# One more head pair transposed by the DMA crossbar in a block-sparse attention + gated conv FFN kernel, with a new written-out order

## The chip, the cores and the metric

One core of a Trainium2 chip. The metric is the device time of one execution in microseconds (us), as the median of several runs.

## The reference: what is computed

Attention with a block mask over q, k, v of shape [4 batches, 8 heads, 768 tokens, 64], then a feed-forward block on the result. The shape of the work, cut to what matters:

```python
scores = (1 / sqrt(64)) * q @ k^T                    # masked to -1e9 outside the allowed 32x32 blocks
attn   = softmax(scores)                             # window, first/last block row and column, 3 sampled blocks
x      = (attn @ v) as [4, 768, 8*64]
h      = relu(x @ w_in)                              # 512 -> 1024
gate   = sigmoid(conv over 3 tokens of h, per channel)
out    = (h * gate) @ w_out                          # 1024 -> 512
```

The kernel computes all 768 x 768 scores; the mask is added inside the score product by 24 extra rows (one for each block of 32 tokens) under the 64 rows of head data, which is why the score products read 88 partitions.

## The kernel before, in words

**Pairs.** The 32 (batch, head) combinations are handled as 16 *pairs* of two heads, four pairs to a batch. A pair's q and k must stand transposed (head dimension on the partitions) in a slot `t` (`T_t`, five slots, [88, 24, 128]): rows 0 to 63 are data, rows 64 to 87 the mask. Columns 0 to 11 hold q, 12 to 23 hold k.

There are two ways to fill a slot. Pairs below `NPE` (line 136) go by `kq_transposes` (line 429 on): TensorE transposes k (six products of 128 columns, L475), the first half of q (three, L537) and later, from a separate load `nq`, the second half of q (three more, L537), each into a PSUM bank `mix`, and copies on DVE or ACT (L328, L324) carry them into the slot. Pairs from `NPE` on go by `kq_crossbar` (line 568 on): k and all of q are loaded into `nat`, the SP queue issues two crossbar transposes (L612, `DMA_TRANSPOSE`) into a staging tile `stg` (two of them), and two copies of 64x1536 on DVE (t<-stg, L328) fill the slot. For such a pair the mask rows stand in another order, so SP also issues one DMA that turns them (t<-mback), from a tile `mback` that two earlier DMAs on SP filled.

**Units.** The score work is cut into 144 units of eight 128x128 blocks. In a unit TensorE makes the scores (S, L774) into one of two PSUM tiles `st`, ACT takes the exponential of all 1024 columns (L786) into `pt` (six buffers), and TensorE multiplies with v (AV, L811, eight products of 65 columns) into `av`. After every few units DVE normalises (`rcp` L720, `xtok` L722), the result is transposed to `xT` by TensorE (L741) or the crossbar (L731), and the feed-forward work runs: f1 = x @ w_in (L919) into `mix`, relu on ACT (L939) or DVE (L941) into `hE`, three multiplications (L977) and two additions (L985) for the conv on DVE, tanh on ACT (L1024), +1 (L1027) and the gate product (L1032, `gT`) on DVE, f2 = gated h @ w_out (L849) into `mix`, eviction to `o2s` (L324 on ACT, L328 on DVE) and the store by SP (L862). A store of a block that is listed in `OUT_TWO` is issued as two DMAs.

**The head.** While the first loads run, TensorE makes 13 warm-up products of 256 columns and 29 *fills* of 128 columns (L230, `warm`) at points where it would wait. DVE builds the mask: it needs the sampled block numbers (`sbi`), makes `A` and `mtok` (L296) and copies mask rows into slot 0. It also sets the column of ones that stands beside each v slot (`v_one`, memset of `vt`, L372, one for each of five slots) and copies q and k into the slot. The first q and k are loaded as float32 and cast: the second q cast, that of head 1, is done by POOL (L326 CAST). POOL also issues the casting loads of the other pairs (L239).

**What sets the order.** All operations are recorded in a graph, but nothing schedules them when the program is built: the text `ORDER` lists every operation in the order in which it is emitted, with the engine where there is a choice and the number of each buffer. Each engine runs its own instructions in that order. An operation that waits holds up all that stand behind it on its engine. `SEQ` is the chain of POOL's middle loads (nq5 is the second half of pair 5's q).

Of the kernel before, what the change touches and what calls it, by code (L numbers as in the profile page):

```python
# [20 lines left out]
0J1f0O0I0K1k0L0002103040M05010P1W01X060Q1U0070R281080S0+A1EA21CA1FA29090/V13G150N181b0a1g0b1h0c1i0d1j0e0U0f0V0g0XV  # L21
1G01HA00YV12G1DG16G2610h1M10i0j0k1NV1IV0l1J01KA191c1LV0m0n0o0p5b05c5g15h0q0r1O00s5d05i10T1PV0t0u1Y11ZV11+V0v5l05m
5n20w1/020V21V1VV05q15r5v00x0y5s35w5x40z5e05f5j5E15F5k1m10A0W0ZV1n1Q02m32n22114V5G55J05K2a00B0C2bV25L00D5O10E5P2d1
0F0G5o5T02cV5Q12eV2fV27V12k22g22y02A24V2B4W2u31w4X2M14Y2O01x4Z2P4+5U5p5t0H5V25u5y5A06015B616231R05z15H6501SV1TV66
2o16742pV32qV5I6a16b2r05M5N5R6f06g2sV2tV6c52lV25S5W5X6k16l5C1230630645Y11l1d24V25V5Z5DV02zV36h06m16t06u68696y16z6d
6v26e6i6A36j6D06E5+02h16n6o16I16J6F46w6x6B6R06C6S6G6H6K56L6M6W16X6T06Y15/V6p22iV2jV6q6N06r0176O6sV6/06U0706P16V6QV
1a71274175763iR0iS7907aiU1iV7i17j7b42NV4iTV00iWVjd07k51y4/2+26Z6+7n07oiX0iY7s17t7p0jejfjgiZV1501z5130152jh7273i+1i/
7x07y7u1j0A1e103217z22v07G177787H7c7d12wV2xVjl1j712C07l7m7L07Mjn2DV47e12EV7I3ji7N47qj87Q1j9V27r7R2F07v7w7S57f2GV2HV
jm7V07W2Q17A7+17/j107Bjj2RV07X0801870887J08927K7O7P8c18d7Tj27U8h07C2jo2SVjpj3V38e38i7Y2T17Z8m181j408j4jq2/V07D2UV
2VV830330jk08n8o531531A348v0j5j6Vjr8wja1821jbjcVjt2jB384ju8x08a8A18B7E08b8f8g7g18C17hA18F08k8G8l8H28p8K18q8y08L851  # L30
8z8M38P08D8Q8R48E8I8J8N8X18Y8r2jD86V8sjw8t18O7FVjvjC8uVjs35VjxjE8Z58S90091jJ0951969208T18+jKjP19719a08/9b93jQjy36V
jF541B55370jz9c2jGjA11jH563939i194989j999n09d9ejR9ojL9k43b23c1573a3d9p59s19t9u1583g13i3j23l592I05a3u3k3r8U1jI9f0
38V13hV2jSjTV0jM9x09yjNA19g3eV3fV8V9z3jV1jWjXA9l1jY0jZ9C19Dj+A2J19K09L9mj/0k09E09P19Q9q9M29R49r9v2KVkh0kik1Vkk2LVkj
9w9U09V9A9B9Fk209H2kl9W59Ik3k4Akp1km9G09Z19+9/1kqa50k51k809Nk9k63n08W23v02W1krknk7Vksa6kaAa739Oaa19Sabac0ke02X19T
af0ag9Xkf9Yak1alah4kx22YVky2ZVkAktam5kb1ap0kca0aqa1a81a9adax1aeaiajay3x3s23w3G3DkukzkdVa21kgVkokvkF3a3kBkwkGkHkIar2
anaz1aoaC0aDaskT1aH1aIat0aAaE3aJ0kCaBaM0aFaNaGl30aU1aKl4aLkUaVaO4aZ0aPaQa+kJkKaW5a/2kDkEkVl5b219h9J3o3z13A3m3a43y4
au0kLkMkWb3l6kXA2b433pV3BVl7V3avb70lc1b8ldb90l903CV3qVbc1aX1labdaYlbV14leAbe53H13E03J3I3S3P3Q13T33Vbk0blli1b0lf0bm1
b1ljb5lkAlx0aR2lyaSlAlzlBlglhA5lF1lH3tV3b6bp1bqbr4ball1bu0bblC3L1jOkYl83M3W0aw03K0aT3Ubvlo0lmlnV6bz1bw2bAbfbg0lpbn
bolqAbB3bsbH0lr1bIbtbxlsbM1bybNlu0bJ0ltA7lGlN2lOlQlDbR0bCbSlvkN1bO5bh1lIbilwV3FV43NVlE1lJlV3bW1bXbT1bY4kZ0bDkOb/0
bK13RA0bE0lPbFlWlRc0c71c8c13k+bLbPbQbUk/bVbZb+c90lKcc0cdkPl0ce53Xl1A1bGbjl2jUlYlLlXlZkQc2c30cach1cbcikRV2lS3+41422  # L40
3/24643lMc42lTl+l/3OVlUcj2m70m11cm0cnm8m2cu1cvcw1co4m3m9m03YV1mambV3cz1m4m5V1cAcfcB3cE0mg0cFmhmd13ZVc540V1miVcG0me
# [71 lines left out]
def kernel(  # L113
# [28 lines left out]

# [76 lines left out]
    OUT_TWO = ((0, 1), (0, 2), (1, 0), (1, 1), (1, 2))  # L219
# [679 lines left out]
    for n, (b, g, tok, C, _) in enumerate(SEGS):  # L899
# [4 lines left out]
        w1 = 128 * C  # L904
# [176 lines left out]
```

## Time and profile before

| | us |
|---|---|
| median of 3 runs | 206.12 |
| lowest, highest run | 205.99, 206.56 |
| the profiled execution | 205.24 |
| its span, first to last instruction | 203.5 |
| time of the profiled execution outside its span | 1.7 |

The profiled execution was 0.88 us faster than the median. Times in the trace are counted from the start of the span. The matmul rows overlap: a product of 128 columns is shown with about 0.22 us, but the next one starts 0.055 us later, so what a product costs TensorE is read from start to start. TensorE's granted clock is 1.000 of full speed.

### The profile page before, as it was taken

To read this page: it belongs to the slowest core of one execution; us is meant where nothing else is said; L and a number is where in the kernel's file an instruction comes from. 1 tells how busy PE (TensorE), PEld (TensorE's weight loads), DVE (VectorE), ACT (ScalarE), POOL (GpSimd) and SP (SyncE) were. 2 spreads that over 40 slices of the span, in tenths; PEclk is the share of its full clock that TensorE was granted. 3 is DMA by queue.
4 is the path that set the end of the run, shared out by engine and by line. 5 is a ranking of instruction groups with operands and counts; after the bars stand their busy time and mean duration, and the time that the engine had idled before them with its cause. 6 is when DMAs were issued, how large, how long until landed. Compare 5 with 4: busy or idle time off the path is not lost.

```text
span 203.5 us, 6346 instructions
## 1 busy us (share of the span) xinstructions
PE 198.4 (98%) x2442; PEld 144.5 (71%) x2442; DVE 183.7 (90%) x576; ACT 189.2 (93%) x251; POOL 68.0 (33%) x148
## 2 busy tenths in 40 slices
PE   7899999999999999999999999999999999999994
PEld 5688878887677766766477676766667657887773
DVE  7789789999999998999899998999999988999961
ACT  6899999999999999999799998999999989998861
POOL 8995646434271504114115443873000000000000
DMA  6999999999789996999948799994005222000315
GB/s 140 178 169 199 184 201 159 159 154 149 72 92 176 113 140 88 241 143 136 175 60 109 138 148 155 186 216 91 0 30 177 82 75 99 3 0 5 133 46 185
DMA packets 50986, 25.45 MB, mean 125 GB/s; under 512 B 35588, under 2 KB 48884, under 8 KB 50956
## 3 DMA queue, kind: packets, MB, share of 16 engines
q0 software_dynamic: 20000, 11.24, 43.6%
q1 hardware_dynamic: 30632, 13.63, 33.2%
q8 instruction: 19, 0.31, 0.6%
q10 hardware_dynamic: 324, 0.18, 0.3%
q14 instruction: 11, 0.09, 0.1%
HBM read 23.09 MB, written 6.29 MB: 144 GB/s over the span
## 4 chain that ended last, share of the span: by engine, by line
PE 93%; DVE 3%; ACT 2%; issue 1%
PE st L774 31%; PE mix L919 21%; PE mix L849 19%; PE av L811 17%; PE mix L741 1%; PE st L849 1%; DVE t L328 1%; PE mix L537 1%; PE mix L475 1%; ACT o2s L324 1%; PE av L996 1%; ACT m L1024 1%; PE av L230 1%; ACT pt L786 1%; DVE mtok L296 0%
## 5 line engine op out<-in xcount | busy, mean ns | idle before, releaser
L786 ACT ACTIVATE pt<-st 128x1024 bf16<-128x1024 f32 x144 | 140.6, 1032 | 3.3 <-PE st L774 2.2
L774 PE MATMUL st<-t 88*128 88x256 bf16 (+2 forms) x600 | 93.3, 267 | 0.8 <-ACT pt L786 0.4
L811 PEld LDWEIGHTS <-pt 128*128 128x128 bf16 x1152 | 55.7, 97 | 12.4
L811 PE MATMUL av<-vt,pt 128*128 128x65 bf16 x1152 | 62.7, 193 | 0.0
L774 PEld LDWEIGHTS <-t 88*128 88x128 bf16 x600 | 48.0, 97 | 20.5 <-DVE t L328 1.0
L919 PE MATMUL mix<-xT,winb 128*128 128x384 bf16 (+2 forms) x288 | 55.2, 307 | 0.1
L977 DVE TENSOR_SCALAR m<-hE,cw 128x382 bf16<-128x382 bf16 (+2 forms) x192 | 50.2, 318 | 0.3 <-ACT hE L939 0.2
L849 PE MATMUL mix<-woutb,gT 128*128 128x512 bf16 (+2 forms) x200 | 49.4, 360 | 0.0
L985 DVE TENSOR_TENSOR m<-m 128x764 bf16<-128x764 bf16 (+2 forms) x64 | 33.6, 531 | 0.2
L919 PEld LDWEIGHTS <-winb 128*128 128x128 bf16 x288 | 23.7, 97 | 8.5 <-issue 0.5
L1024 ACT ACTIVATE m<-m 128x764 bf16<-128x764 bf16 (+2 forms) x32 | 26.3, 825 | 0.1
L849 PEld LDWEIGHTS <-gT 128*128 128x128 bf16 x224 | 18.8, 97 | 9.0 <-DVE gT L1032 0.3
L420 POOL COPY pace<-pt 1x1 bf16<-1x1 bf16 x24 | 8.4, 348 | 50.0 <-ACT pt L786 49.8
L939 ACT ACTIVATE hE<-mix 128x384 bf16<-128x384 f32 (+2 forms) x37 | 18.1, 502 | 0.6 <-PE mix L919 0.4
L1032 DVE TENSOR_TENSOR gT<-m,hE 128x764 bf16<-128x764 bf16 (+3 forms) x36 | 18.1, 510 | 0.7 <-ACT hE L939 0.4
L722 DVE TENSOR_TENSOR xtok<-av,rcp 128x384 bf16<-128x384 f32 (+2 forms) x36 | 18.2, 508 | 0.4
L239 POOL DMA_DIRECT2D nat<-in_q_dram x23 | 17.0, 739 | 3.1 <-issue 2.2
L941 DVE TENSOR_SCALAR hE<-mix 128x384 bf16<-128x384 f32 x27 | 15.0, 554 | 2.6 <-PE mix L919 2.3
L328 DVE COPY t<-mix 64x384 bf16<-64x384 bf16 (+1 forms) x34 | 14.0, 411 | 1.6 <-PE mix L475 0.6
L1027 DVE TENSOR_SCALAR m<-m 128x764 bf16<-128x764 bf16 (+3 forms) x36 | 12.0, 336 | 1.2 <-ACT m L1024 0.9
L324 ACT COPY o2s<-mix 128x512 f32<-128x512 f32 (+2 forms) x17 | 9.3, 549 | 3.8 <-PE mix L849 3.7
L239 POOL DMA_DIRECT2D vn<-in_v_dram x16 | 12.0, 748 | 0.9 <-issue 0.3
(76 smaller groups left out, 124.6 us busy)
## 6 DMA issues: line engine op xcount, KB each, us to landing
out_dram<-o2s SPq DMA_DIRECT2D x16, 256.0 KB
vn<-in_v_dram POOLq DMA_DIRECT2D x16, 192.0 KB, 5.0
nat<-in_k_dram POOLq DMA_DIRECT2D x15, 192.0 KB, 4.6
out_dram<-o2s SPq DMA_DIRECT2D x15, 128.0 KB
nat<-in_q_dram POOLq DMA_DIRECT2D x6, 192.0 KB, 4.2
winb<-in_moe_w_in_dram POOLq DMA_DIRECT2D x2, 512.0 KB, 7.2
woutb<-in_moe_w_out_dram POOLq DMA_DIRECT2D x4, 256.0 KB, 6.8
nat<-in_q_dram POOLq DMA_DIRECT2D x9, 96.0 KB, 5.3
```

Source lines behind the costliest of these rows:

```text
L239: return op(name, {eng: occ}, lambda e: on(e).dma_start(out=dst(), in_=src), prio, deps, dma=(kind, service), **kw)
L722: nm = op("norm", {"DVE": t_dps(128 * C)}, lambda e: nc.vector.tensor_tensor(out=xtok_t[xk.index][:, 0:C].rearrange("p c h d -> p h c d"), ...
L774: nc.tensor.matmul(out=st[:, 128 * x:128 * (x + n_)], lhsT=t[0:88, 12 + 6 * hh + kc, :], rhs=t[0:88, idx:idx + (n_ - 1) * (2 if P < NPE el ...
L786: nc.scalar.activation(out=pt_t[ptb.index][:, c0:c1], in_=st_t[stb.index][:, c0:c1], func=AF.Exp, bias=0.0, scale=0.125)
L811: nc.tensor.matmul(out=o[:, off:off + 65], lhsT=pt_t[ptb.index][:, 128 * x:128 * x + 128], rhs=V_t[vslot_b[P].index][:, hh, kc, 0:65], sta ...
L849: nc.tensor.matmul(out=acc(), lhsT=gT_t[gb.index][:, ffc, 128 * t:128 * t + 128], rhs=woutb[:, ffc, c0:c1], start=(ffc == 0), stop=(ffc == ...
L919: nc.tensor.matmul(out=mix_t[hb.index][:, w1 * y:w1 * y + w1], lhsT=winb[:, fc, 128 * ffc:128 * ffc + 128], rhs=xT_t[xt_buf[n].index][:, f ...
L939: nc.scalar.activation(out=dst, in_=src, func=AF.Relu, bias=0.0, scale=0.5)
L977: nc.vector.tensor_scalar(out=m_t[cb.index][:, x, y, 0:w], in0=hE_t[heb.index][:, f0 + y, t0 + x:t0 + x + w], scalar1=cw[:, x, f0 + y:f0 + ...
L985: nc.vector.tensor_tensor(out=m[:, a_, :, 0:w], in0=m[:, a_, :, 0:w], in1=m[:, b_, :, 0:w], op=ALU.add)
L1024: th = [op("tanh", {"ACT": t_act(2 * w) + 0.04}, lambda e, cb=cb, w=w: nc.scalar.activation(out=m_t[cb.index][:, 0, :, 0:w], in_=m_t[cb.in ...
L1032: nc.vector.tensor_tensor(out=gT_t[gtb.index][:, f0:f0 + 2, t0:t1], in0=m_t[cb.index][:, 0, :, 0:w], in1=hE_t[heb.index][:, f0:f0 + 2, 1 + ...
```

## The change

1. `NPE` goes from 6 to 5: pair 5 goes by `kq_crossbar`, and `nq5` leaves `SEQ`.
2. `OUT_TWO` loses (1, 1) and (1, 2): those two stores are one DMA each.
3. `ORDER` is written anew from the first line on.

```diff
-    NF, NPE = 4, 6
+    NF, NPE = 4, 5
...
-    SEQ = "nq0 nq1 nq2 k4 q4 nq3 v4 k5 q5 w0 v5 w1 k6 q6 w2 w3 v6 k7 q7 v7 nq4 nq5"
+    SEQ = "nq0 nq1 nq2 k4 q4 nq3 v4 k5 q5 w0 v5 w1 k6 q6 w2 w3 v6 k7 q7 v7 nq4"
...
-    OUT_TWO = ((0, 1), (0, 2), (1, 0), (1, 1), (1, 2))
+    OUT_TWO = ((0, 1), (0, 2), (1, 0))
...
-0J1f0O0I0K1k0L0002103040M05010P1W01X060Q1U0070R281080S0+A1EA21CA1FA29090/V13G150N181b0a1g0b1h0c1i0d1j0e0U0f0V0g0XV
+0J1f0O0I0K1k0L0002103040M05010P1W01X060Q1U0070R281080S0+A1EA21CA1FA090/V13G150N181b0a0b0c0d0e0U0f0V0g0XV1G01HA00YV
...
```

What the new order does on the engines, counted over the whole program: TensorE has 12 transposes and their 12 weight loads fewer; DVE makes six `t<-mix` copies fewer (four of 64x384, two of 64x768), two more `t<-stg` and one more `vt<-vn`, and one relu fewer; ACT makes one relu more and the copy `vt<-vn` no longer; SP issues two crossbar transposes more and two stores fewer (with both halves of a store counted). Three places that the prediction speaks of follow, with a fourth in a sentence; `+` and `-` mark rows that only the changed or only the old kernel has there.

On DVE, at the very head: `nblk` and the first mask rows of slot 0, then the four later memsets of ones (`vt1` to `vt4`), `A` and `mtok` from the sampled blocks `sbi`, and below, after the first copies into slot 0 (the row with `av0` is one of them):

```order
 L328 COPY t0_67<-nblk_125 24x3x128
-L372 MEMSET vt1_73 128x12
-L372 MEMSET vt2_74 128x12
-L372 MEMSET vt3_75 128x12
-L372 MEMSET vt4_76 128x12
 L296 SCALAR_TENSOR_TENSOR A_130<-sbi_126,keyid_129,A_130 24x24 x2
 L296 SCALAR_TENSOR_TENSOR mtok_131<-sbi_126,keyid_129,A_130 24x384
```

The four memsets moved behind the mask and the first copies into the slot; they now stand ahead of the copy of head 1's first q.

On POOL, at the head: loads of pair 0's v (`vn0`) and of pair 2's k (`nat1`), two copies of mask rows inside slot 0, the cast of head 1's q of pair 0 (`nat2<-o2s0`) and the load of pair 2's q:

```order
 L239 DMA vn0_87<-in_v_dram 128x2x384
 L239 DMA nat1_80<-in_k_dram 128x2x384
-L239 DMA nat1_80<-in_q_dram 128x2x192
 L326 COPY t0_67<-t0_67 24x768
 L326 COPY t0_67<-t0_67 24x3x128
 L326 CAST nat2_81<-o2s0_113 128x192
+L239 DMA nat1_80<-in_q_dram 128x2x192
 L326 COPY t1_68<-t0_67 24x6x128
```

The load's issue moved behind the cast; the copies and the cast moved up by one issue.

On SP, in the first third, pair 5's crossbar transpose of k (`stg0<-nat0`) now stands ahead of the last mask copy (slot 4) and of the two DMAs that fill `mback`, that of its q behind them, and the turn of its mask rows (`t0<-mback`) behind the first crossbar transpose of pair 6.

On DVE, around the first use of pairs 10 and 11: four copies from the staging tiles into slots `t0` and `t1`, among the +1 rows (L1027, which wait for ACT's tanh), the gate products (L1032) and evictions to `o2s`. Before, where slot 0 holds pair 10:

```order
L1027 TENSOR_SCALAR m2_109<-m2_109 128x2x382
L1027 TENSOR_SCALAR m3_110<-m3_110 128x2x382
L328 COPY t0_67<-stg1_78 64x12x128
L1032 TENSOR_TENSOR gT1_112<-m2_109,hE1_106 128x2x382
L1032 TENSOR_TENSOR gT1_112<-m3_110,hE1_106 128x2x382
L328 COPY t1_68<-stg0_77 64x12x128
L328 COPY o2s3_116<-mix0_65 128x512
```

And now, where slot 1 holds pair 10:

```order
L1027 TENSOR_SCALAR m2_109<-m2_109 128x2x382
L328 COPY vt0_72<-vn1_88 128x12x64
L720 RECIPROCAL rcp0_99<-av0_63 128x6
L328 COPY t0_67<-stg0_77 64x12x128
L328 COPY t1_68<-stg1_78 64x12x128
L1032 TENSOR_TENSOR gT1_112<-m2_109,hE1_106 128x2x382
L328 COPY t1_68<-stg1_78 64x12x128
L1027 TENSOR_SCALAR m3_110<-m3_110 128x2x382
```

The last copy for pair 10 stood behind the +1 row of `m3`; it now stands ahead of it, but behind pair 11's first copy.

More of the change, by code (lines that the diff above doesn't have):

```diff
@@ L20 @@
 ORDER = """
-0J1f0O0I0K1k0L0002103040M05010P1W01X060Q1U0070R281080S0+A1EA21CA1FA29090/V13G150N181b0a1g0b1h0c1i0d1j0e0U0f0V0g0XV
[L22 to L40, printed above, removed]
@@ L61 @@
+qT0hPi71i8hQqoquqPAgqvqy1qUqzi95hI1qpqAr20qwhR2qxqVAhhJr4r3hSri2rjr5qBqK0qLhY0hZi01i1qCA3qMAii30i21iaibhK1hLA2i4qQ0
+i51qRi6AqSAjic1qW1rlqXr6idrkqZqYra3q+rbrcqE1qFhT0qGhUAie0qHifAqIA0rI0rJrKArO1rPq/r0rdr1rQAr7rU0rVrL0rMrNArR1s21rSs3
+rW1rTArq0rZ0r8rerfqJqDpzopr9rmrXrYrw1r+s40rnr/1s5rgrhrxrrs71ros0s1rpsA0s8s93sasu1rsrysvsBsbs6rzrtswrAA0ruA3sc1sxsC
+rC0sDrDrEsyA2rFsdsEArGArBszrvsFrHsesfsi0sjskslso1sgA1shsmAsnspsqsrssAst
 """
```

55 lines of the change are left out of this document (35 added, 20 removed).

## The prediction

> **What bounds the kernel now.** I read the page first, then the stretches by time, then the chain of work that ended last, and last the instructions around the places where that chain leaves TensorE.
>
> ```profile
> PE 198.4 (98%) x2442; PEld 144.5 (71%) x2442; DVE 183.7 (90%) x576; ACT 189.2 (93%) x251; POOL 68.0 (33%) x148
> PE 93%; DVE 3%; ACT 2%; issue 1%
> ```
>
> TensorE (PE) is busy for 98% of the 203.5 us span, and 93% of the chain that ended last is its work. But ACT at 93% and DVE at 90% leave little room, so the shares alone do not say who sets the pace. The next rows are from the view of stretches: start and end, length, then busy time with number of instructions for PE, weight loads, DVE, ACT and POOL, the granted clock, the DMA share and GB/s.
>
> ```profile
> 8.50:24.50 16.00, 15.55 (x265) 13.24 (x263) 13.37 (x39) 15.94 (x17) 12.60 (x23) 1.00 1.28 186
> 24.50:45.00 20.50, 20.48 (x291) 15.91 (x289) 18.96 (x55) 20.36 (x25) 8.94 (x20) 1.00 1.21 170
> 45.00:90.00 45.00, 45.00 (x550) 31.89 (x549) 43.21 (x127) 44.68 (x56) 14.97 (x28) 1.00 1.02 136
> 90.00:180.00 90.00, 89.77 (x1055) 62.15 (x1054) 85.21 (x265) 86.46 (x114) 24.05 (x63) 1.00 0.61 108
> ```
>
> From 8.5 to 45 us ACT is full (15.94 of 16.00, 20.36 of 20.50): the exponentials run back to back. From 45 to 180 us TensorE is full and ACT has 3.9 us to spare (135.00 less 44.68 and 86.46). So work taken from TensorE pays in full only where it is the bound, and a start of the exponentials that comes sooner pays in the first part. The chain by time says where it leaves TensorE: up to 9.6 us in the head, at the end, and in between at one place alone (start, length, what):
>
> ```profile
> 94.56 0.57 ACT o2s L324
> 95.12 0.40 ACT m L1024
> 95.75 0.85 ACT m L1024
> 96.62 0.36 DVE m L1027
> 97.01 0.81 DVE t L328
> 97.86 0.33 PEld L774 LDWEIGHTS <-t 88*128 88x128 bf16 x4 [0.72 <-DVE t L328]
> 97.87 0.61 PE L774 MATMUL st<-t 88*128 88x384 bf16 x4 [0.23 <-DVE t L328]
> 98.58 1.02 ACT L786 ACTIVATE pt<-st 128x1024 bf16<-128x1024 f32 x1 [1.07 <-PE st L774]
> ```
>
> The last three rows are from the timeline, with the idle time before them in brackets. Pair 10's last copy into its slot (97.01) stands on DVE behind a +1 row that waits for tanh. The scores wait for the copy, with 0.23 us of TensorE idle, and ACT then idles for 1.07 us.
>
> **Part 1: pair 5 leaves TensorE.** The transposes that go, in the timeline of TensorE, each followed by what starts next:
>
> ```profile
> 35.76 0.50 PE L475 MATMUL mix<-ident,nat 128*128 128x128 bf16 x6
> 36.10 0.28 PE L811 MATMUL av<-vt,pt 128*128 128x65 bf16 x4
> 39.62 0.33 PE L537 MATMUL mix<-ident,nat 128*128 128x128 bf16 x3
> 39.78 0.28 PE L811 MATMUL av<-vt,pt 128*128 128x65 bf16 x4
> 57.40 0.33 PE L537 MATMUL mix<-ident,nq 128*128 128x128 bf16 x3
> 57.56 0.60 PE L774 MATMUL st<-t 88*128 88x256 bf16 x4
> ```
>
> From start to next start they take 36.10 - 35.76 = 0.34, 39.78 - 39.62 = 0.16 and 57.56 - 57.40 = 0.16 us: **0.66 us** of TensorE. Nine of the twelve lie ahead of 45 us, where ACT is the bound; there the room lets TensorE take feed-forward products forward, which are then missing from the full stretch behind. I take all 0.66 us; the ends are 0 (ACT keeps the pace and nothing is taken forward) and 0.66.
>
> The Trainium skill speaks against this part: the page "VectorE: DVE Perf Modes", section "Rules for kernel authors", says to transpose 128x128 on TensorE where PSUM will do, and its section "The three transpose paths" gives 390 ns there and 1309 ns on the crossbar. By 390 ns the twelve would be 4.7 us of TensorE, an estimate from that page; the trace's 0.055 us from start to start decides against counting so.
>
> The copies change too:
>
> ```profile
> L328 DVE COPY t<-stg 64x1536 bf16<-64x1536 bf16 x20 | 11.6, 586 | 0.2
> L328 DVE COPY t<-mix 64x384 bf16<-64x384 bf16 x24 | 8.4, 351 | 0.8 <-PE mix L537 0.4
> L328 DVE COPY t<-mix 64x768 bf16<-64x768 bf16 x10 | 5.5, 555 | 0.8 <-PE mix L475 0.6
> L324 ACT COPY vt<-vn 128x768 bf16<-128x768 bf16 x1 | 0.8, 837 | 0.0
> ```
>
> DVE loses four of 351 ns and two of 555 ns and gets two of 586 ns: 1.40 + 1.11 - 1.17 = 1.34 us less. ACT loses one copy of 837 ns to DVE. The other moves between the two are single relus and evictions, and nearly cancel. So no engine gets more work; I count nothing for these, since neither is the bound where TensorE is full, and they are the cover for the rest of the new order.
>
> On SP and the DMA engines two crossbar transposes come in. Their cover is time. The first row below is the first crossbar transpose of pair 6, the second the first score product that reads pair 5's slot, the third all crossbar transposes of that line (min, median, max of the issue in ns):
>
> ```profile
> 34.41 3.38 SPq L612 DMA_TRANSPOSE stg<-nat  x2
> 45.60 0.38 PE L774 MATMUL st<-t 88*128 88x128 bf16 x2
> L612 SPq DMA_TRANSPOSE stg<-nat x20: 1210/1237/2307, 34.4 to 138.1; - x20
> ```
>
> The last thing that pair 5 now needs from SP, the turn of its mask rows, stands right behind pair 6's first transpose, so it is issued at about 34.41 + 1.24 = 35.7 us, and 45.60 - 35.7 = 9.9 us are left for its way and for two copies of 0.59 us. I cost it at nothing; what it costs when that cover is gone is the rival below.
>
> **Part 2: the head.** The chain there, and what POOL does beside it:
>
> ```profile
> 3.54 0.23 DVE vt L372 x4
> 3.80 0.26 DVE A L296
> ...
> 5.89 1.03 PE st L774 x8
> ...
> 7.04 0.03 issue
> 7.06 0.35 PE av L515 x3
> ...
> 8.56 1.03 ACT pt L786
> 4.50 0.72 POOL L239 DMA_DIRECT2D nat<-in_q_dram  x1
> 5.26 1.34 POOL L326 COPY t<-t 24x768 bf16<-24x768 bf16 x2
> 6.67 0.34 POOL L326 CAST nat<-o2s 128x192 bf16<-128x192 f32 x1
> ```
>
> The four memsets of ones stand on the chain itself, and `A` is not shown waiting for its load, so without them the mask, the copies into slot 0, the first scores (5.89) and the first exponential come 0.23 us sooner. It could be nothing, if the load of the block numbers landed just before 3.80, or 0.26 with the gap between rows; I take 0.23. The second step must not eat it: unit 2 needs head 1's q, whose transposes (7.06) wait for POOL's cast (ends 7.01). The issue of 0.72 us that goes behind the cast lets the cast end up to 0.72 sooner; the two fills that now stand behind the score products of units 0 and 1 run into the time that this leaves. TensorE reaches these transposes 0.23 sooner and finds the data there. The memsets now run on DVE before head 1's copy, in time in which DVE waits for those transposes. So all exponentials of the full stretch begin **0.23 us** sooner.
>
> The load that moved is pair 2's q. Its landing, in us after its issue, that of nine other loads of its size, and its first use:
>
> ```profile
> nat<-in_q_dram POOLq DMA_DIRECT2D x1, 96.0 KB, 7.0
> nat<-in_q_dram POOLq DMA_DIRECT2D x9, 96.0 KB, 5.3
> 12.98 0.33 PE L537 MATMUL mix<-ident,nat 128*128 128x128 bf16 x3
> ```
>
> It landed at 4.50 + 7.0 = 11.5, and is now issued behind two copies and a cast, at 4.50 + 1.34 + 0.34 and the gaps, about 6.3. If the 7.0 us were its own, it would land at 13.3 and TensorE, which now comes by at 12.75, would stand for 0.55 us; if it is the queue of loads ahead of it, it lands at 11.5 as before. Nine loads of that size take 5.3 us in the median, so part of the 7.0 is queue, and with 6.3 + 5.3 = 11.6 it would be there in time: I take 0, and keep 0.55 for the range.
>
> **Part 3: the rest.** At pair 10 the copy no longer waits for the last tanh, but has pair 11's copy of 0.59 us ahead of it in place of a +1 of 0.36. The gain ends at the 0.23 us that TensorE idled, the loss at the 0.59 us of that copy; I take 0. Two stores as one DMA each: SP waits most of the time, nothing. The other hundreds of moves I can't price one by one; since each engine has less work and TensorE's stream is otherwise the same, I take 0 and keep 0.6 us on either side, the size of the one hole that the chain shows (0.23 on TensorE, 1.07 on ACT; about the mean of the two).
>
> **Sum.** 0.66 + 0.23 = 0.89 us less than the profiled execution: 205.24 - 0.89 = 204.35 us, span 202.6. The median of the runs shown is 0.88 above that execution, so 206.12 - 0.89 = **205.2 us**.
>
> **The rivals.**
>
> *ACT keeps the pace.* Most of pair 5's transposes lie where ACT is full, and if the new order takes no other TensorE work forward, the 0.66 is lost: 206.12 - 0.23 = 205.9 us. For it speaks the full ACT up to 45 us; against it that 0.16 us of them lie behind, and that ACT gets no more work while TensorE's part behind 45 us is a fixed sum from which each product done earlier is taken.
>
> *A slot comes late through SP (slower).* SP issues in order, and a store or a transpose that waits holds up every crossbar transpose behind it. The view of waits shows how long:
>
> ```profile
> SPq L862 <- ACT o2s L324: 21.7, 8, 12.1
> ```
>
> Eight waits of stores for an eviction, the longest 12.1 us. With two transposes more and another order on SP, such a wait can now stand ahead of a pair's transposes or of its mask rows. From a wait of 9.9 us on, the cover worked out above for pair 5, each us of it is a us that TensorE stands; at 12.1 it is 12.1 - 9.9 = 2.2 us, and 205.2 + 2.2 = 207.4 us. Against it speaks that such waits lay ahead of transposes before too, and no slot came late.
>
> *More than the sum.* If the new order also closes the hole at 97 us and some of what ACT lost there, up to 0.6 us more goes: 204.6 us.
>
> **How the numbers follow.** The forecast has 0.47, more than the sum 0.15, ACT's pace 0.20, the late slot or another hole of its size 0.18. 0.3% is 0.62 us here, about what a measurement of this kernel can tell from no change: faster means below 205.5 us. The first two cases make faster 0.62, the third the same 0.20, the last slower 0.18. The range reaches down to 205.2 - 0.6 - 0.5 = 204.1 (the unknown moves and the spread of the three runs, 0.57) and up to 206.9, where the 0.66 is lost, pair 2's q costs its 0.55 and 0.6 us of new waits come in (205.9 + 0.55 + 0.6 = 207.05, of which I leave out the last bit); that leaves out most of the late slot.
>
> **What would show it.** No L475 or L537 rows between 36 and 42 us, and no three L537 rows near 57 us; `A` at about 3.55 us, the first scores at 5.65, the first exponential at 6.3; TensorE's L537 for pair 2 without idle time at about 12.75; no wait of L774 for t<-stg before 60 us; the stretch from 45 to 180 us shorter for the same units. Wrong would be: `A` still at 3.8, an idle TensorE behind a crossbar copy, or ACT idle for more than a us anywhere between 10 and 180 us.

## The result, and the profile after

The changed kernel is slower: 207.25 us as the median of 22 executions (204.72 to 212.21) beside 205.86 for the kernel before (205.33 to 206.75). The ratio is 1.0034, with a 95% interval of 1.0018 to 1.0051. Like all ratios below it leaves out executions more than 1.5% above the fastest of the same kernel; the eight of the changed kernel that go by this (208.38 to 212.21) ran at a granted clock of 0.99 to 1.00, so they belong to what the change costs, and the plain quotient of the two medians is 1.0068.

The changed kernel also spreads over 7.5 us, the one before over 1.4. The profiled execution took 209.0 us, its span 207.2. Busy times and the chain that ended last, from its page:

```profile
PE 198.7 (96%) x2430; PEld 144.1 (70%) x2430; DVE 181.7 (88%) x572; ACT 189.9 (92%) x251; POOL 67.1 (32%) x146
...
PE 65%; DMA 18%; DVE 11%; issue 2%; ACT 2%; POOL 1%; SPq 0%; DVEq 0%; POOLq 0%
...
L328 DVE COPY t<-stg 64x1536 bf16<-64x1536 bf16 x22 | 12.0, 549 | 3.2 <-DMA stg<-nat 2.9
```

The counts are as they were worked out: 12 products fewer on TensorE, four instructions fewer on DVE. What is new stands in the second row: of the chain, 18% are now DMA, and TensorE has 65% in place of 93%. The third row is the copy from the staging tile on DVE, which now stands idle for 2.9 us in all, at two places, because a crossbar transpose has not landed.

The same stretches as before, in the same columns:

```profile
8.50:24.50 16.00, 15.53 (x263) 13.13 (x260) 14.11 (x38) 15.89 (x18) 13.06 (x26) 1.00 1.34 194
24.50:45.00 20.50, 19.73 (x268) 15.05 (x265) 16.70 (x48) 19.90 (x24) 7.17 (x17) 1.00 1.35 153
45.00:90.00 45.00, 43.97 (x554) 31.48 (x552) 42.53 (x126) 43.23 (x55) 17.34 (x41) 1.00 1.07 151
90.00:180.00 90.00, 87.99 (x1023) 60.60 (x1022) 81.93 (x253) 84.80 (x109) 22.44 (x48) 1.00 0.65 105
```

TensorE is no longer full in any of the last three: it lacks 0.77, 1.03 and 2.01 us, where it lacked 0.02, 0.00 and 0.23. The second last column, the DMA share, is the time of all packets over the time of the core's 16 DMA engines; it passes 1 where packets overlap. Below, "full" DMA engines are those of the first two stretches, where it is 1.2 and more. Where TensorE stood, the view of what it waited for says (us in all, how often, the longest). The first and the last row stand in the kernel before too:

```profile
PE av L230 <- DVE warm L223: 1.2, 1, 1.2
PE mix L919 <- DMA xT<-xtok: 1.0, 1, 1.0
PE st L774 <- DMA t<-mback: 1.0, 1, 1.0
PE mix L919 <- DVE hE L941: 0.9, 1, 0.9
PE mix L919 <- DVE t L328: 0.7, 1, 0.7
PE st L774 <- ACT pt L786: 0.4, 1, 0.4
```

The four new waits come to 3.6 us, and 209.0 - 3.6 = 205.4 us is what is left. Two of them stand at pair 5, in rows of the timelines of DVE and TensorE:

```profile
40.70 0.55 DVE L328 COPY t<-stg 64x1536 bf16<-64x1536 bf16 x1 [1.14 <-DMA stg<-nat]
...
42.19 0.48 PE L919 MATMUL mix<-xT,winb 128*128 128x384 bf16 x2 [0.69 <-DVE t L328]
...
48.00 0.38 PE L774 MATMUL st<-t 88*128 88x384 bf16 x2 [0.99 <-DMA t<-mback]
```

Pair 5's copy waits 1.14 us for its crossbar transpose; a copy out of a PSUM bank stands behind it on DVE (41.77 us in the chain), and f1 waits 0.69 for that bank. Later the scores stand 0.99 us for the turn of pair 5's mask rows. SP's own rows show how that came:

```profile
25.13 1.40 SPq L612 DMA_TRANSPOSE stg<-nat  x1
26.63 0.81 SPq L239 DMA_DIRECT2D t<-t  x1
27.50 1.62 SPq L340 DMA_DIRECT2D mback<-t  x2
29.57 2.48 SPq L612 DMA_TRANSPOSE stg<-nat  x1
39.02 0.81 SPq L239 DMA_DIRECT2D t<-mback  x1
40.91 1.23 SPq L612 DMA_TRANSPOSE stg<-nat  x1
42.24 0.81 SPq L239 DMA_DIRECT2D t<-mback  x1
```

The first transpose of pair 5 waits for its k until 25.13, and behind it stand the fills of `mback` (27.50; before they were issued at 13.03). The transpose of its q, issued at 29.57, is shown in the chain with 11.03 us until it lands at 40.60. The turn of pair 5's mask rows is the last row, at 42.24, behind pair 6's first transpose at 40.91; it lands 5.71 us later, at 47.95. The prediction had put these two at 34.41 and 35.7. Pair 6's transpose waits for pair 6's load of k. Its landing, in us after its issue at 30.1 (changed) and at 30.5 (before), is the row on which most of what follows hangs:

```profile
nat<-in_k_dram POOLq DMA_DIRECT2D x1, 192.0 KB, 10.8
```

```profile
nat<-in_k_dram POOLq DMA_DIRECT2D x1, 192.0 KB, 3.9
```

### The profile page after: what moved, and what is told of

It is laid out like the page before. It is cut to its first block, busy times and chain, and to the rows that moved or that the text cites. A ratio compares the mean times of both kernels' runs of the same rounds, so it can differ in the third digit from the quotient of the medians.

```text
span 207.2 us, 6306 instructions
## 1 busy us (share of the span) xinstructions
PE 198.7 (96%) x2430; PEld 144.1 (70%) x2430; DVE 181.7 (88%) x572; ACT 189.9 (92%) x251; POOL 67.1 (32%) x146
## 4 chain that ended last, share of the span: by engine, by line
PE 65%; DMA 18%; DVE 11%; issue 2%; ACT 2%; POOL 1%; SPq 0%; DVEq 0%; POOLq 0%
PE st L774 20%; PE mix L849 16%; PE mix L919 14%; PE av L811 10%; DMA stg<-nat 8%; DMA nat<-in_q_dram 7%; DMA t<-mback 3%; DVE t L328 2%; DVE m L985 2%; DVE m L977 2%; ACT pt L786 1%; PE st L849 1%; DVE hE L941 1%; DVE xtok L722 1%; PE av L996 1%
## 5 line engine op out<-in xcount | busy, mean ns | idle before, releaser
L786 ACT ACTIVATE pt<-st 128x1024 bf16<-128x1024 f32 x144 | 140.2, 1034 | 4.3 <-PE st L774 3.4
L811 PEld LDWEIGHTS <-pt 128*128 128x128 bf16 x1152 | 54.9, 97 | 12.9
L811 PE MATMUL av<-vt,pt 128*128 128x65 bf16 x1152 | 61.7, 193 | 0.0
L420 POOL COPY pace<-pt 1x1 bf16<-1x1 bf16 x24 | 8.9, 372 | 43.8 <-ACT pt L786 42.2
L941 DVE TENSOR_SCALAR hE<-mix 128x384 bf16<-128x384 f32 x26 | 14.3, 554 | 7.2 <-PE mix L919 7.0
L1032 DVE TENSOR_TENSOR gT<-m,hE 128x764 bf16<-128x764 bf16 (+3 forms) x36 | 18.2, 511 | 0.4
L239 POOL DMA_DIRECT2D nat<-in_q_dram x23 | 17.7, 770 | 2.0 <-issue 1.9
L328 DVE COPY t<-stg 64x1536 bf16<-64x1536 bf16 x22 | 12.0, 549 | 3.2 <-DMA stg<-nat 2.9
L328 DVE COPY t<-mix 64x384 bf16<-64x384 bf16 (+1 forms) x28 | 11.5, 410 | 1.8 <-PE mix L475 0.8
L1027 DVE TENSOR_SCALAR m<-m 128x764 bf16<-128x764 bf16 (+3 forms) x36 | 11.8, 332 | 1.2 <-ACT m L1024 0.7
L239 POOL DMA_DIRECT2D vn<-in_v_dram x16 | 11.4, 715 | 2.9 <-DVE vt L328 1.7
```

Source lines behind the costliest of these rows:

```text
L239: return op(name, {eng: occ}, lambda e: on(e).dma_start(out=dst(), in_=src), prio, deps, dma=(kind, service), **kw)
L328: nc.vector.tensor_copy(out=dst, in_=src)
L786: nc.scalar.activation(out=pt_t[ptb.index][:, c0:c1], in_=st_t[stb.index][:, c0:c1], func=AF.Exp, bias=0.0, scale=0.125)
L811: nc.tensor.matmul(out=o[:, off:off + 65], lhsT=pt_t[ptb.index][:, 128 * x:128 * x + 128], rhs=V_t[vslot_b[P].index][:, hh, kc, 0:65], sta ...
```

## The experiments

**The theories.** *A: the landing.* Two crossbar transposes among full DMA engines delay the loads and DMAs around them by microseconds, and with the order in which SP has its instructions this makes slots late. *B: DVE's order*: the copies hold up what stands behind them. *C: the head*: moving the load or the memsets costs what the transposes gain. *D: nothing but the transposes on TensorE counts*, so they gain less than the sum or nothing. Each experiment is one part of the change done to the kernel before, or one part of it undone. The rows with `+` and `-` are the instructions in order on the engine named.

### The memsets alone: h_ones

The kernel before, with only the four memsets of ones moved, on DVE:

```diff
-L372 MEMSET vt_73 128x12
-L372 MEMSET vt_74 128x12
-L372 MEMSET vt_75 128x12
-L372 MEMSET vt_76 128x12
 L296 SCALAR_TENSOR_TENSOR A<-sbi,keyid,A 24x24 x2
...
 L286 CAST ident_123<-ident 24x24
+L372 MEMSET vt_73 128x12
...
 L328 COPY t_67<-av_63 64x3x128
```

> The kernel before with only the four memsets of ones moved behind the first copies into slot 0; POOL's load stays in front. Port theory (a DVE copy from SBUF waits while a copy of POOL is running): A at 3.47, the copy from mtok starts at about 4.68 and takes 0.32 since POOL's copy starts only at 5.26, first scores at 5.56 in place of 5.89, third exponential at 8.2 to 8.3 in place of 8.56; the time 0.2 to 0.3 us lower (ratio 0.9985 to 0.999). Rival (the head is held by something else that the memsets hide): first scores stay at 5.8 to 5.9, ratio 1.000.

Measured: 205.73 us (205.13 to 206.13) beside 205.68, ratio 1.0002 (0.999 to 1.0013). `A` comes at 3.47 in place of 3.80, as the prediction had it, yet the first scores come at 6.52 us, later than the 5.89 of before. TensorE's rows, of this kernel and then of the kernel before, show why:

```profile
4.91 0.53 PE L515 MATMUL mix<-ident,nat 128*64 128x128 bf16 x3
5.37 0.61 PE L230 MATMUL av<-warm 128*128 128x128 bf16 x4
5.77 0.53 PE L475 MATMUL av<-ident,nat 128*128 128x128 bf16 x3
```

```profile
4.75 0.35 PE L515 MATMUL mix<-ident,nat 128*64 128x128 bf16 x3
5.03 0.40 PE L230 MATMUL av<-warm 128*128 128x128 bf16 x4
5.27 0.33 PE L475 MATMUL av<-ident,nat 128*128 128x128 bf16 x3
```

Four products of 128 columns take 5.77 - 5.37 = 0.40 us here, 5.27 - 5.03 = 0.24 there: 0.10 and 0.06 apiece, for the same instructions. So in the first microseconds TensorE goes at about half speed for a time that differs between executions, though the column of the granted clock reads 1.00. The Trainium skill, page "TensorE: Matmul & The Clock Gate", section "What's actually happening", tells of a gate that lets half the clock pass until a window of about 3.4 us has been busy. These rows agree in the factor (0.10 to 0.055 us); when the switch comes varies: in a_sp three products take 0.18 us from 4.38 on, in p5_alone2 four still take 0.42 us from 6.10 on. What the memsets give is thus hidden behind TensorE in some executions, and in the median nothing of it is seen.

### The load alone: h_load

The kernel before, with only the issue of pair 2's q moved behind the second cast on POOL:

```diff
-L239 DMA nat_80<-in_q_dram 128x2x192
 L326 COPY t_67<-t_67 24x768
 L326 COPY t_67<-t_67 24x3x128
 L326 CAST nat_81<-o2s_113 128x192
+L239 DMA nat_80<-in_q_dram 128x2x192
```

> The kernel before with only the issue of pair 2's q moved behind POOL's cast. Port theory: POOL's first copy starts at 4.55, before DVE's copy from mtok (5.01), and holds it to about 5.5; first scores at 6.05 to 6.1 in place of 5.89, third exponential at 8.7 to 8.8; the time 0.2 us higher (ratio 1.001). Rival (the prediction's step: the earlier cast only helps): first scores at 5.89, ratio 1.000 or a little below.

Measured: 205.81 us (205.65 to 206.24), ratio 1.0010 (1.0001 to 1.0019): a loss of about 0.2 us. The move lets POOL's copy of mask rows begin 0.7 us sooner, and there it meets DVE's copies of 24x256. POOL, DVE and the first scores of this kernel, then DVE of the kernel before:

```profile
4.56 1.10 POOL L326 COPY t<-t 24x768 bf16<-24x768 bf16 x1
...
5.01 0.93 DVE L328 COPY t<-mtok 24x256 bf16<-24x256 bf16 x2
...
6.38 1.03 PE L774 MATMUL st<-t 88*128 88x384 bf16 x8 [0.48 <-DVE t L328]
```

```profile
5.01 0.45 DVE L328 COPY t<-mtok 24x256 bf16<-24x256 bf16 x2
```

The two copies on DVE take 0.93 in place of 0.45 us, and the first scores wait for the copy behind them. The changed kernel shows the same (POOL's copy at 4.55, DVE's two at 4.68 with 0.97), and its first scores come at 6.08; in a_all2 below, where the load is back in front, the two take 0.58 us and the first scores come at 5.81. The page "SBUF — State Buffer" of the Trainium skill, section "Who interferes with whom", says that DVE and GpSimd share a pair of ports as an exclusive lock, and that where an instruction of DVE uses the pair, the one that issues first holds the other off; 0.93 beside 0.45 agrees.

### Pair 5 alone, in two orders: p5_alone and p5_alone2

The kernel before with pair 5 by the crossbar and nothing else of the change; SP fills `mback` early and turns pair 5's rows at once.

```diff
-    NF, NPE = 4, 6
+    NF, NPE = 4, 5
...
-    SEQ = "nq0 nq1 nq2 k4 q4 nq3 v4 k5 q5 w0 v5 w1 k6 q6 w2 w3 v6 k7 q7 v7 nq4 nq5"
+    SEQ = "nq0 nq1 nq2 k4 q4 nq3 v4 k5 q5 w0 v5 w1 k6 q6 w2 w3 v6 k7 q7 v7 nq4"
```

> The kernel before with only part 1: pair 5 by the crossbar, in the old order, its transposes right behind the fills of mback on SP, its two copies on DVE just ahead of the unit that first reads the slot. The prediction's term of 0.66 us: ratio 0.9965 to 0.9975. ACT keeps the pace: 0.999 to 1.000. If the crossbar's way is too slow even from there (11 us from issue to landing as in the changed kernel's profile): TensorE idles before unit 40 and the ratio is over 1.003.

Measured: 206.99 us (206.34 to 207.57), ratio 1.0063 (1.0043 to 1.0083). TensorE's timeline has one long new wait, the second row; the first is DVE's:

```profile
43.83 1.11 DVE L328 COPY t<-stg 64x1536 bf16<-64x1536 bf16 x2
...
46.73 0.28 PE L811 MATMUL av<-vt,pt 128*128 128x65 bf16 x4 [1.01 <-DVE xtok L722]
```

Here the two copies from staging stand in one piece ahead of a normalisation (`xtok`). p5_alone2 takes them apart, on DVE:

```diff
+L328 COPY t_67<-stg_78 64x12x128
 L941 TENSOR_SCALAR hE_105<-mix_65 128x384
 L1027 TENSOR_SCALAR m_108<-m_108 128x2x382
+L328 COPY t_67<-stg_78 64x12x128
 L941 TENSOR_SCALAR hE_105<-mix_66 128x384
-L328 COPY t_67<-stg_78 64x12x128 x2
```

> Pair 5 alone by the crossbar in the old order as in p5_alone, but its two copies on DVE apart, in the two gaps of 0.62 and 0.53 us ahead of relus that wait for TensorE, in place of both ahead of the xtok that held TensorE for 1.17 us. If that wait was only the place of the copies, it goes and the ratio comes down by 0.004 to 0.006. Then by the prediction's term of 0.66 us: ratio 0.997; by the rival that ACT keeps the pace up to 45 us: 0.999 to 1.000. If the ratio stays above 1.003, the crossbar's way costs more than its place on DVE.

Measured: 206.29 us (205.69 to 206.67), ratio 1.0025 (1.0011 to 1.0039). The wait is gone, and with it 0.7 us, so B was true of p5_alone. But pair 5 alone, with no such wait left, is still slower than before by 0.25%, outside both forecasts above (0.997, 0.999 to 1.000). TensorE's one new wait (0.20 us, in p5_alone too) is for ACT, behind the place where six of the transposes stood. Below it, the landing of pair 6's k in this kernel:

```profile
36.92 0.60 PE L774 MATMUL st<-t 88*128 88x128 bf16 x4 [0.20 <-ACT pt L786]
```

```profile
nat<-in_k_dram POOLq DMA_DIRECT2D x1, 192.0 KB, 8.2
```

It takes 8.2 us in place of 3.9, but no wait of TensorE in this execution hangs on it. Where the time goes, and that the transposes give so little, is taken up below, at x_twice.

### SP's order undone: a_sp, and the changed kernel again

a_sp is the changed kernel with SP's order mended: the mask copy and the fills of `mback` ahead of pair 5's transposes, and pair 5's turn ahead of pair 6's transpose.

```diff
-L612 DMA_TRANSPOSE stg_77<-nat_79 128x6x128
 L239 DMA t_71<-t_67 24x3072
 L340 DMA mback<-t_67 24x3x128 x2
-L612 DMA_TRANSPOSE stg_77<-nat_79 128x6x128
+L612 DMA_TRANSPOSE stg_77<-nat_79 128x6x128 x2
+L239 DMA t_67<-mback 24x2x768
 L239 DMA t_68<-mback 24x2x768
 L612 DMA_TRANSPOSE stg_78<-nat_80 128x6x128
-L239 DMA t_67<-mback 24x2x768
 L612 DMA_TRANSPOSE stg_78<-nat_80 128x6x128
```

> The changed kernel with one difference on SP: the slot 4 mask copy and the two fills of mback ahead of pair 5's crossbar transposes, and pair 5's mask turn ahead of pair 6's. Theory (pair 5's mask rows come late because these small DMAs stand behind a transpose that waits 16 us for k): the turn is issued by 36 us, TensorE does not wait for t<-mback at 47 us; median 1 to 2 us below the changed kernel's 207.25 (ratio to the kernel before 0.996 to 1.001) and a narrower spread than its 204.7 to 212.2. Rival (the slow crossbar landing of 11 us itself is what makes pair 5 late): a wait of about the same size for t<-stg in its place, ratio 1.003 to 1.006 and the same spread.

Measured: 205.83 us (204.52 to 210.55), ratio 1.0000 (0.9978 to 1.0021), where the change had 1.0034. Both waits at pair 5 are gone:

```profile
13.39 1.63 SPq L340 DMA_DIRECT2D mback<-t  x2
26.61 4.80 SPq L612 DMA_TRANSPOSE stg<-nat  x2
31.72 1.66 SPq L239 DMA_DIRECT2D t<-mback  x2
```

The turn is issued at 31.72 and not at 42.24. The intervals of the two ratios overlap (1.0018 and 1.0021), so the gain in time is likely but not settled by these two; in the traces, both of the change have the wait for pair 5's turn (after_again below), and none of the four kernels with SP's order mended has it. The spread is hardly narrower than the 7.5 us of the change (6.0), and the profiled execution (207.96 us) still waits elsewhere:

```profile
PE mix L919 <- DMA xT<-xtok: 1.3, 1, 1.3
...
PE mix L919 <- DVE hE L941: 0.7, 1, 0.7
```

after_again is the changed kernel once more, to see whether its waits stand still.

> The changed kernel once more, for a second profile, since its first one (209.0 us) lies in the upper part of its runs (204.7 to 212.2). If the waits of TensorE for t<-mback at 47 us, for hE at 41 and 133 us and for xT<-xtok at 124 us are what spreads its times, an execution of 206 to 207 us shows the same places with less time in them, 1 to 3 us less in all; if they are the same size, the spread lies elsewhere.

One execution, 208.4 us. They don't stand still: the wait for pair 5's turn is there again (0.7), those for `xT` (1.0), `hE` (0.9) and the bank (0.7) are not, and two others are, at 60 us for pair 7's slot and at 143 us for an `o2s`:

```profile
PE st L774 <- DVE t L328: 1.8, 1, 1.8
...
PE st L774 <- DMA t<-mback: 0.7, 1, 0.7
PE mix L919 <- ACT o2s L324: 0.5, 1, 0.5
```

They sum to 3.0, and 208.4 - 3.0 = 205.4 us, as in the first execution. Which transfer is waited for differs between the two executions; what is left without the waits does not.

### The later waits, mended one by one: a_sp_mid, a_all, a_all2

a_sp_mid adds two moves to a_sp, against the waits for `xT` and `hE` between 120 and 135 us: on POOL the third part of pair 13's q right behind its second, and on DVE one normalisation ahead of four products of the conv.

```diff
 L239 DMA nat_81<-in_q_dram 128x2x128
+L239 DMA nat_81<-in_q_dram 128x2x64
...
 L239 DMA vn_87<-in_v_dram 128x2x384
-L239 DMA nat_81<-in_q_dram 128x2x64
```

> a_sp with two more moves: the third part of pair 13's q is issued by POOL right behind its second part (111.7 us in place of 117.7), and one xtok on DVE goes ahead of four multiplications (about 1.3 us sooner), so that its crossbar turn into xT is issued sooner. Theory: the waits for xT<-xtok at 122 to 124 us (1.2 to 1.5 us) and for hE behind a copy that waits for stg at 132 us (0.9 to 1.1 us) go; the median comes 0.8 to 2 us below a_sp (205.83), the ratio is 0.990 to 0.996, and the highest run comes below 207.5. Rival (the slow landings only move on to the next transfer): ratio 0.998 to 1.002 and a spread as before, with waits for DMA at other places.

Measured: 206.39 us (205.39 to 211.31), ratio 1.0033 (1.0003 to 1.0063): no gain, and no better than the change itself. The two waits are not in its execution, but neither are they in after_again, which has none of the moves; and the one at 60 us, which a_sp's execution didn't have, is there:

```profile
PE st L774 <- DVE t L328: 2.1, 1, 2.1
```

So what I expected of the time fell, and the rival is nearer: without these waits, another is there. a_all undoes the head's load as well, on POOL:

```diff
+L239 DMA nat_80<-in_q_dram 128x2x192
 L326 COPY t_67<-t_67 24x768
 L326 COPY t_67<-t_67 24x3x128
 L326 CAST nat_81<-o2s_113 128x192
-L239 DMA nat_80<-in_q_dram 128x2x192
```

> a_sp_mid with the issue of pair 2's q back ahead of POOL's first mask copy, as in the kernel before, and the memsets of ones where the change put them. Port theory: POOL's copy starts at 5.27, DVE's from mtok takes about 0.3 us, the first scores start 0.3 to 0.5 us sooner than in a_sp_mid where TensorE is warm by then; the ratio 0.001 to 0.0025 below a_sp_mid. Rival (TensorE's slow products set the start of the scores anyway): no difference.

Measured: 205.59 us (204.38 to 208.08), ratio 0.9986 (0.9968 to 1.0003). That is 0.0047 below a_sp_mid, more than the 0.001 to 0.0025 expected, but the two intervals touch (1.0003), so the size is not settled. The wait at pair 7 was still there in the profiled execution (206.68 us), and the one for `o2s` at 141 us too:

```profile
PE st L774 <- DVE t L328: 0.8, 1, 0.8
PE mix L919 <- ACT o2s L324: 0.7, 1, 0.7
```

a_all2 meets both: on POOL (first rows) pair 7's k and q are issued ahead of pair 6's v, and on SP (last rows) a store is issued ahead of crossbar transposes that it stood behind, so that its `o2s` comes free sooner.

```diff
-L239 DMA vn_87<-in_v_dram 128x2x384
 L686 COPY pace<-woutb 1x1
 L239 DMA nat_82<-in_k_dram 128x2x384
 L686 COPY pace<-woutb 1x1
 L239 DMA nat_82<-in_q_dram 128x4x192
+L239 DMA vn_87<-in_v_dram 128x2x384
...
+L862 DMA out_dram<-o2s_116 128x512
 L612 DMA_TRANSPOSE stg_78<-nat_80 128x6x128
...
 L862 DMA out_dram<-o2s_113 128x256 x2
-L862 DMA out_dram<-o2s_116 128x512
```

> a_all with the two places that still waited in its profile mended: POOL issues pair 7's k and q ahead of pair 6's v (pair 7's q at about 43 to 44 us in place of 46.3), and the store of the o2s tile that ACT waited for at 140 us goes on SP ahead of a crossbar transpose (at about 124 us in place of 135). Theory (the changed order has its waits where a slot or a buffer that comes through a DMA has little slack, and the 12 transposes are worth a few tenths where nothing waits): no wait of TensorE over 0.5 us between 10 and 190 us, median 204.2 to 205.0, ratio 0.993 to 0.997, spread under 2 us. Rival (the order as such is too tight and a wait turns up at another place): ratio 0.997 to 1.002 with a spread as in a_all (204.4 to 208.1).

Measured: **205.21 us** (204.59 to 205.60 and one execution of 253.67; nine in all) beside 205.73, ratio 0.9976 (0.9963 to 0.9989). This version is 0.24% faster than the kernel before, and its interval lies clear of the changed kernel's too; without the one long execution its spread (1.0 us) is as narrow as that of the kernel before. The gain is short of the 0.993 to 0.997 expected, and by the ratio alone the rival's 0.997 to 1.002 holds; the waits and the spread came out as the theory had them. What TensorE waits for is down to the two old rows:

```profile
PE av L230 <- DVE warm L223: 1.2, 1, 1.2
PE st L774 <- ACT pt L786: 0.4, 1, 0.4
```

Pair 6's k still takes 9.0 us to land in it. So the late landing is not cured; no wait of TensorE behind it is left in this execution.

### Is it the transposes, or the bytes? x_xbar and x_q96

The change puts two things on the DMA engines at 20 to 30 us: two crossbar transposes, and all of pair 5's q (192 KB) in one early load in place of half of it. x_xbar is the kernel before with two idle crossbar transposes into a staging tile, whose results are overwritten:

```diff
         for g in range(2):
             nc.sync.dma_start(out=mback[64:88, g], in_=T_t[0][64:88, g:g + 5:2])
+        for x in range(2):
+            nc.sync.dma_start_transpose(out=stg_t[1][:, x].rearrange("p h c s -> p (h c) s"), in_=nat_t[0][:, 1])
```

> The kernel before with two extra crossbar transposes of pair 5's k on SP, into a staging tile that is filled anew later, at the place where p5_alone has pair 5's; TensorE keeps its transposes, so nothing is saved. If the crossbar transposes themselves hold up the other transfers: POOL's waits for the loads of pair 6 and of the third and fourth part of w_out are longer, the last of these is issued at 38 to 41 us in place of 35, pair 7's q at 45 to 47 in place of 43 to 46, ratio 1.000 to 1.003. If they do not: these issues stay where they are, ratio 1.000.

x_q96 is the kernel before with 96 KB of loading more at 22 us: pair 5's first load of q takes both halves.

```diff
+                     lq.fn = lq.fn if P != 5 else (lambda e: [on(e).dma_start(out=nat_t[nb.index][:, 0].rearrange("p (g h c) -> p h g c", g=2, h=2)[:, hh], in_=q[b, h0 + hh].rearrange("(g p c) d -> p g (c d)", g=2, p=128)) for hh in range(2)])
```

> The kernel before, with all of pair 5's q loaded where its first half is loaded (two loads of 96 KB at 22 us; the second half is not used and the later load stays). If the 96 KB more in the stretch in which the DMA engines are full hold up the loads behind them: the fourth part of w_out is issued at 37 us or later in place of 35. If it is the crossbar transposes that do it, it stays at 35 to 36. Ratio 1.000 to 1.002 by both.

Measured: x_xbar 206.36 us (205.84 to 210.84), ratio 1.0051 (1.0024 to 1.0078); x_q96 205.62 us (205.21 to 206.18 beside the profiled one), ratio 0.9997 (0.9986 to 1.0008). The 96 KB cost nothing that can be measured, and the transposes cost 0.5%, more than the 0.000 to 0.003 expected. The trace of x_q96 is at a granted clock of 0.854 (227.62 us), so only its early landings and issues are read. POOL's rows around the fourth part of w_out, of x_xbar and of the kernel before; `pace` are copies of one element by which POOL waits for an earlier load:

```profile
38.26 0.27 POOL L686 COPY pace<-nat 1x1 bf16<-1x1 bf16 x1 [0.58 <-DMA nat<-in_k_dram]
38.70 0.72 POOL L239 DMA_DIRECT2D woutb<-in_moe_w_out_dram  x1 [0.17 <-issue]
```

```profile
34.67 0.18 POOL L686 COPY pace<-nat 1x1 bf16<-1x1 bf16 x1
34.96 0.72 POOL L239 DMA_DIRECT2D woutb<-in_moe_w_out_dram  x1
```

The load is issued at 38.70 us in place of 34.96, because pair 6's k landed late; in x_q96 it is issued at 35.87. The landing of that k, issued between 29.9 and 31.2 us, as the view of DMA issues gives it for the profiled execution of each kernel:

| | us from issue to landing |
|---|---|
| before, h_ones, h_load, x_twice, x_q96 (no crossbar transpose before 34 us) | 3.9, 4.3, 4.2, 3.9, 4.5 |
| x_xbar (two of no use) | 7.0 |
| p5_alone, p5_alone2 | 7.9, 8.2 |
| a_sp, a_sp_mid, a_all, a_all2 | 8.4, 9.5, 9.7, 9.0 |
| the change, after_again (and SP's order of the change) | 10.8, 10.6 |

The two groups don't overlap, and x_q96 stands with those without. This is what bears the first half of theory A, that the transposes make the load land late.

The two transposes move 384 KB of their own, four times what x_q96 adds, and an ordinary transfer of that size was not tried. That their bytes are the cause is not likely, though. The stretch from 24.5 to 45 us in x_xbar:

```profile
24.50:45.00 20.50, 20.48 (x288) 15.97 (x285) 18.85 (x54) 20.36 (x25) 7.63 (x16) 1.00 1.37 157
```

The share is 1.37 with 157 GB/s, where the kernel before has 1.21 with 170. Over all traces it is 1.20 to 1.29 without the transposes and 1.33 to 1.39 with them, while the GB/s (144 to 170 and 153 to 174) hardly differ: the packets take more time, and hardly more is moved.

How x_xbar then loses its 0.5% the trace does not show. Its execution of 206.24 us has no wait of TensorE over 0.2 us between 10 us and the end that the kernel before has not. Of the 1.0 us that it is longer, 0.49 are there at an exponential that starts at 20.26 us (19.77 before), ahead of the transposes' issue at 27.19, and 0.33 come at the end of the program (table in the next section). That late landings cost TensorE time is seen in the changed kernel, not here.

### What the twelve transposes are worth: x_twice

The kernel before, with pair 5's twelve transposes on TensorE made twice in place:

```diff
-                o.fn(e)
+                [o.fn(e) for _ in range(2 if ops.index(o) in (180, 183, 187) else 1)]
```

> The kernel before, with pair 5's twelve transposes on TensorE made twice in place, nothing else; what the second set costs is what taking one set away can bring at most. The prediction's term (0.055 us each, all of it on the path): 0.66 us, ratio 1.0032. The rival that ACT keeps the pace up to 45 us: only the three at 57 us count, 0.16 us, ratio 1.0005 to 1.001.

Measured: 206.25 us (205.82 to 206.93), ratio 1.0025 (1.0011 to 1.0039), that is 0.23 to 0.80 us for twelve more. Where it falls is read from the starts of the exponentials (the first columns of the rows of L786: the third, the 41st, and the last, the 144th) and from the last eviction to `o2s` by ACT, in us:

| | start of 3rd | 3rd to 41st | 41st to 144th | last `o2s` to end of span |
|---|---|---|---|---|
| before | 8.56 | 37.86 | 138.48 | 2.87 |
| x_twice | 9.39 | 38.24 | 138.56 | 2.86 |
| h_ones | 9.10 | 37.93 | 138.59 | 2.85 |
| x_xbar | 8.58 | 38.33 | 138.65 | 3.20 |
| p5_alone2 | 9.26 | 37.96 | 138.32 | 3.53 |
| the change | 8.76 | 39.71 | 140.23 | 2.82 |
| a_all2 | 8.50 | 37.86 | 138.30 | 2.91 |

Nine of the twelve stand between the 3rd and the 41st exponential, three behind it. Each row is one execution. Between kernels with the same order there, before, h_ones and h_load (37.97 and 138.52), the time from the 3rd to the 41st differs by 0.11 us, and so does the time behind it. Made twice the twelve cost 0.38 us ahead of the 41st (nine at 0.055 would be 0.50); 0.29 of it comes at one exponential, that of 36.94 us before, right behind the first six. The 0.08 behind comes ahead of the last three, and h_ones has it too. Taken away, in p5_alone2 and a_all2, they give nothing ahead of the 41st (37.96 and 37.86 beside 37.86) and 0.16 to 0.18 us behind (138.32 and 138.30 beside 138.48; p5_alone has 138.30). In p5_alone and p5_alone2, whose exponentials stand in the order of before, 0.11 of it comes between 57.65 and 63.93 us of before, right behind the last three. More work and less work are not mirror images: ACT sets the pace of the first stretch, so TensorE can fall behind it there but not run ahead; the 0.20 us that it waits for ACT at 36.92 in p5_alone2 is the same thing seen from the other side.

The table also says where the traced execution of p5_alone2, with a span 1.3 us longer than before (204.8 beside 203.5), loses its time: 0.70 in the head, which has the instructions of before and comes as late in x_twice (9.39), and 0.66 behind the last eviction. In between it loses nothing.

## Why the prediction was wrong

The forecast was 205.2 us, in a range of 204.1 to 206.9, and faster by over 0.3%; measured are 207.25 us, above the range, and slower by 0.34%. At the measured ratio the 206.12 us of the runs shown would be 206.8, inside the range by a hair and on the wrong side.

**The step that failed**, in its own words: on SP and the DMA engines "two crossbar transposes come in. Their cover is time", with the turn of the mask rows "issued at about 34.41 + 1.24 = 35.7 us, and 45.60 - 35.7 = 9.9 us are left", and "I cost it at nothing". Two things in it failed. The 34.41 was taken as fixed, though it is itself the landing of a load: that landing comes 6.9 us later in the changed kernel (10.8 in place of 3.9), and 3.1 us later with two transposes alone (x_xbar), 4.0 to 4.3 with pair 5 alone (p5_alone, p5_alone2). So the turn was issued at 42.24, its way of 5.71 us ended at 47.95, and TensorE stood 0.99 us for it. And for pair 5's own crossbar transposes no landing was counted at all: the second took 11.03 us, DVE waited 1.14 us for it, and f1 0.69 us for what stood behind on DVE. That is 1.7 us where the prediction had nothing. The prediction's own rows showed a DMA share of 1.28 and 1.21 up to 45 us; I read that column for neither stretch.

**A second term** was sized at nothing: the "other hundreds of moves", taken as 0 with 0.6 us on either side. The two waits at 124 and 134 us (1.9 us together) are not in p5_alone2, which has pair 5 by the crossbar in the old order and twelve executions within 1.0 us, so they come with the new one. Which of its moves brings them is not shown; in a_all2, with SP's order mended and three loads, a store and a normalisation moved, no such wait is left and the executions but one lie within 1.0 us.

**The rival that came true** is the late slot (0.18), in place and sign. Its mechanism was near, not the same: I let a store's wait for an eviction hold SP up from 9.9 us on, and it was waits for loads. Its argument against, that no slot came late before, did not carry over to a kernel in which the loads land later.

**TensorE's 0.66 us.** The term was mis-sized: 0.16 to 0.18 us come, about those of the three transposes behind 45 us. For the nine others the rival "ACT keeps the pace" was right, and what I held against it, that TensorE takes other products forward into the room, does not show in a_all2.

**The head's 0.23 us.** `A` came at 3.47, sooner than the 3.55 forecast. But the second step did eat it: the load moved behind the cast, costed at 0 with an end of +0.55 for a late landing, costs about 0.2 us by another way, POOL's earlier copy in the way of DVE's. And the memsets alone gave 1.0002 (0.999 to 1.0013), with TensorE's own start setting the first scores in the profiled execution (6.52 us). The head was 0.2 longer in the changed kernel (8.76 beside 8.56 for the third exponential) where I had -0.23; but with the head of before this start lies anywhere from 8.56 to 9.39 in the traces, so these two executions alone tell nothing, and it is h_load's ratio that shows the loss. The end of +0.55 did not come: TensorE's products for pair 2 stand at 13.19 us without idle time.

**More than the sum.** The idle TensorE at 97 us is gone in a_all2, as that rival had it; what it brings there is not told apart from the transposes. The merged stores were not tried apart.

**The sum as measured** for the two profiled executions: 209.0 - 205.24 = 3.8 us, of which the four new waits are 3.6 and the head 0.2, with 0.2 gained on TensorE; 0.2 is left unexplained. In the median the loss is smaller; the waits differ from execution to execution.

**What stays open**: why the same wait comes in one execution of a kernel and not in another, how the median of x_xbar loses its 0.5%, and the end of the three kernels that have two more transposes on SP and the stores of before. Their last stretch is 3.53 (p5_alone2), 3.20 (x_xbar) and 3.18 us (p5_alone) in place of 2.87. SP's last wait for the stores is one of 1.4 us in p5_alone2 and three of 1.1 in all before; that two more DMAs on SP change which wait comes last is only argued. The change itself, with two stores fewer, does not have this.

## What to carry to other kernels

Read the DMA share of the stretch before giving TensorE's work to the DMA engines. Here, at 1.2 to 1.3, two crossbar transposes made another load late, though 96 KB of ordinary loads did not; so the cover must be counted from issue to landing, at the slowest landing in the rows, and for every load that lands behind it. Then look what stands behind each late landing on an in-order queue, and move that, as a_all2 does: here the work could stay on the DMA engines once TensorE no longer waited for what stood behind it. And work taken from TensorE paid only in the stretch in which it was the bound, though the same work added cost in the other.

## What the hardware showed that was not expected

- With two crossbar transposes of 128x768 that nobody reads, issued at 27 to 31 us, a load of 192 KB issued beside them landed after 7.0 us (3.9 to 4.5 in five kernels without), and the kernel took 0.5% longer; 96 KB of ordinary loads more did nothing that could be measured (0.9997).
- A crossbar transpose took 11.03 us from issue to landing in a stretch with a DMA share of 1.35, and the issues of the three in that trace's rows took 1.2 to 2.5 us.
- In the first microseconds products of 128 columns start 0.10 us apart, then 0.055, and the switch lies before 4.4 us in a_sp and past 6.1 us in p5_alone2, at a granted clock shown as 1.00.
- With a copy on POOL 0.7 us earlier, two small copies on DVE took 0.93 us in place of 0.45.
